# A fused attention and MLP block on one core: where the normed x is spilled, when Q is loaded, and how far the row maxima run ahead

## The chip, the cores and the metric

The kernel runs on one core of a Trainium2 chip. Its time is device microseconds (us) of the program; lower is better. The engines are named as in the profile: PE (TensorE matmul), PEld (its weight loads), DVE (VectorE), ACT (ScalarE), POOL (GpSimd) and SP (SyncE, which here issues nearly all DMA transfers, in order). SPq is the issuing side of SP.

## The reference

All in fp32, with x of [1, 2048, 512], 32 heads of 16, and an MLP of width 1792:

```python
def reference(A_x, A_wqkv, A_wo, B_x, B_w1, B_b1, B_w2, B_b2):
    xn = _layernorm(A_x)                                  # (x - mean) / sqrt(var + 1e-5)
    # attention on xn
    qkv = (xn @ A_wqkv)   # -> q, k, v, each [32 heads, 2048, 16]
    p = softmax(q @ k.T * 16 ** -0.5)
    s = (p @ v, heads joined) @ A_wo
    # MLP on xn
    h = relu(xn @ B_w1 + B_b1) ** 2
    g = silu(h @ B_w2 + B_b2)
    return A_x + s * g
```

## The kernel before

**Numbers.** Every fp32 operand is split into a high and a low part, and a product is three matmuls (high by high, high by low, low by high). On most tiles POOL makes the split (lines 93 and 94: the high part, then the remainder); some are split by ACT and DVE (99 and 100). Matmuls of the later stages use 64 rows of the array each, and two of them, on the upper and the lower half, run at the same time: such a couple is called a pair here, and a half a side or lane.

**Stages.** (1) To about 64 us: x is loaded, normed and transposed into four tiles `xT` (one for each 512 tokens, both parts, 2 MB each), and the first projections run. (2) The lead, from 64 to about 182 us: the other projections (V, Q, K). The function `side_rounds` walks through 390 rounds; a round is one matmul on each side; a projection tile takes 12 rounds a side, and the lower side runs 18 rounds behind. `single` puts extra matmuls between the rounds: 'm' is one tile of scores of which DVE takes the row maxima (line 321), 's' is one tile of exponentials on ACT (1195). The lists `ROUND_MM`, `ROUND_MS` and `ROUND_SM` say in which rounds. (3) The loop over 512 slots, 16 for each of 32 units (a unit is 4 heads by 512 queries). A slot has four tiles of exponentials, four of maxima for later units, the product with V (384) and a share of the MLP's matmuls (252) in groups of four slots ("long slots"), eight chunks of 256 tokens, 56 slots each. (4) From slot 452: the output projection (220), then the end.

**The maxima.** For the softmax the maxima over keys of a unit are taken ahead of its exponentials; `LEAD` = 24 slots separate the two, and each side takes 32 maxima a unit. Once a unit's 64 are there, `max_end` reduces them (329), and six slots later `shift` (351 to 354, on DVE) transposes and negates them; they go to DRAM (360) and come back (375) into two rows of the unit's Q tile, so that the score matmul subtracts them.

**A projection tile of Q or K** goes PSUM, ACT copy `raw` (1000, two buffers), POOL split into `hl` (93, 94, three buffers), then two DMA stores, one of the high and one of the low part (938). A V tile goes through ACT to `vt` (1040, seven buffers) and a store (1043). The order of SP, ACT, DVE and POOL is fixed by the order of the calls; `later(n, fn)` puts a call off by n steps: in the lead a step is six rounds, in the loop a slot.

**DMA around the change.** `load_q_pair` loads one Q tile with six DMAs of 32 KB (147); `qm` tiles serve the maxima (a ring of three), `qe` tiles the exponentials (four). `max_end(g)` calls it at set slots of each unit. The normed x is written from `xT` to DRAM in eight spills of 1 MB (1355), at every third slot count g of the lead, and is read back for the MLP by `load_xc` (497), as two DMAs for each chunk:

```python
            if s in (7, 8):
                load_q_pair(u, "qe", s - 7, qes.setdefault(u, []))
            if s in (5, 7) and u + 1 < NU:
                load_q_pair(u + 1, "qm", (s - 5) // 2, qms.setdefault(u + 1, []))
```

The first xc can only be loaded when the lead's last matmul has read `xT`, whose memory it takes. In the tail `wo_load` brings the attention outputs `oc` (667). POOL normalises a unit's outputs in slot 12 of the next unit (422 to 424), from a list of slots called `EVAC`.

Of the kernel before, what the change touches and what calls it, by code (L numbers as in the profile page):

```python
# [9 lines left out]
F32 = mybir.dt.float32  # L10
# [7 lines left out]
P = 128  # L18
S = 2048
D = 512  # L20
# [3 lines left out]
KO = D // P  # L24
# [3 lines left out]
NU = NQ * 4  # L28
LEAD = 24
CW = 256  # L30
# [5 lines left out]
EVAC_LAST = (1, 3, 4, 5, 7, 9)  # L36
GAPS = (18, 19, 20, 22)
FIRST = 2
LAST_MAX = 486
TWO = (2, 3, 452, 453)  # L40
ROUND_MM = [12 * k for k in range(1, 32)] + [12 * k + 6 for k in range(2, 22)]
ROUND_MS = [12 * k + 6 for k in (22, 23, 25, 26, 28, 29)]
ROUND_SM = [12 * k + 6 for k in (24, 27, 30)]
AHEAD = (
# [7 lines left out]
def kernel(  # L52
# [11 lines left out]
    nc = tc.nc  # L64
# [11 lines left out]
    xn_d = dram.tile([2, P, KO, S], F32, name="xn_d")  # L76
# [9 lines left out]
    b1_t = const.tile([P, FO], F32, name="b1_t")  # L86
    b2_t = const.tile([P, D], F32, name="b2_t")
# [21 lines left out]
    with ExitStack() as ph:  # L109
# [31 lines left out]
        qms = {}  # L141
        qes = {}
# [182 lines left out]
        def max_end(g):  # L325
            for u in [u for u, n in left.items() if n == 0]:
                del left[u]
                m4 = m4s[u % 2]
                nc.vector.tensor_reduce(m4[:, :16], mxs[u], axis=AX.X, op=ALU.max)
                mxs[u] = m4  # L330
                late.append((g + (6 if u else 2), u))
            u, s = divmod(g, 16)
            if u >= NU:
                return
            qd, qc = divmod(u, 4)
            if qc == 2 and qd + 1 < NQ and s % 2 == 0:
                load_k(qd + 1, s // 2)
            if qc == 3 and qd + 1 < NQ and s % 2 == 0 and s < 8:
                load_k(qd + 1, 8 + s // 2)
            if s in (7, 8):  # L340
                load_q_pair(u, "qe", s - 7, qes.setdefault(u, []))
            if s in (5, 7) and u + 1 < NU:
                load_q_pair(u + 1, "qm", (s - 5) // 2, qms.setdefault(u + 1, []))

        def shift_due(g):
            if late and late[0][0] <= g:
# [117 lines left out]
        def mlp_tasks(mp):  # L464
# [28 lines left out]

            def load_xc(c):
                    xc = xp.tile([P, 2, KO, CW], F32R, name="xc")
                    for i in range(2):
                        nc.sync.dma_start(
                            xc[:, i].bitcast(F32), xn_d[i, :, :, c * CW : (c + 1) * CW]
                        )
                    state["xc"] = xc  # L500

            def first_pair(c, f):
# [397 lines left out]
        st = right(ln, "wq_st", 1)  # L900
# [7 lines left out]
        xTs = {c: cp.tile([P, 2, KO, 512], F32R, name=f"xT{c}") for c in (3, 0, 1, 2)}  # L908
# [25 lines left out]
        def qk_store(m, c, hl):  # L934
            cs = slice(c * 512, (c + 1) * 512)
            dst = q_d[m] if m < 4 else k_d[m - 4]
            for i in range(2):
                nc.sync.dma_start(dst[i, :, cs], hl[:, i].bitcast(F32))

        def qk_terms(m, c, ps):  # L940
            wq, m0 = wq_cols(m)
# [217 lines left out]
        order = []  # L1159
# [58 lines left out]
        for i in range(NT + 3):  # L1218
            if i in (2, 3):

                kos = slice(2 * i - 4, 2 * i - 2)
# [35 lines left out]
            if i >= 7 and (i - 3) % 4 == 3:  # L1257
                c = (i - 3) // 4
# [3 lines left out]
            if i >= 3 and (i - 3) % 4 == 3:  # L1262
                c = (i - 3) // 4
# [48 lines left out]
        def lead_rounds():  # L1312
            for i in side_rounds(specs, single):
                if i % 6 == 0:
                    now[0] = i // 6
                    run_waiting()
                kinds = "mm" if i in ROUND_MM else "ms" if i in ROUND_MS else "sm" if i in ROUND_SM else ""
                uses = [single(lane, kind) for lane, kind in enumerate(kinds)]
                if i % (3 * KO) == 0 and uses:
                    since[0] = uses[0]  # L1320
                if i == 6 * KO:
                    since[1] = uses[1]
                yield

        rounds = lead_rounds()
        for g in range(LEAD):
            shift_due(g)
            while min(made) < 2 * g + 2:
                next(rounds)
            max_end(g)  # L1330
            if g == 0:
                raw_r = [load_w("wv", 3 * P, ((D + P, 3 * P),))]
            if g == 3:
                for ko in range(KO):
                    split_w(wr_t, ko, slice(3 * P, 6 * P), raw_r[0][:, ko])
                ln.close()
                pools["v"] = ph.enter_context(tc.tile_pool(name="vp", bufs=1))
            if g == 12:
                s1.close()
                ep = ph.enter_context(tc.tile_pool(name="ep", bufs=1))  # L1340
                rot["pt"] = [ep.tile([P, 512], F32, name=f"pt{i}") for i in range(NPT)]
                pools["n"] = ph.enter_context(tc.tile_pool(name="np", bufs=1))
                mlp_early()
            if g in (18, 20):
                split_w1((g - 18) // 2)
                load_w1(3 + (g - 18) // 2)
            if g == 16:
                for fo in range(3):
                    load_w1(fo)
                load_v(0)  # L1350
                nc.sync.dma_start(b1_t, b1.rearrange("(fo p) -> p fo", p=P), allow_slow_non_contiguous=True)
                nc.sync.dma_start(b2_t, b2[None, :].to_broadcast([P, D]))
            if g % 3 == 2:
                c, i = divmod(g // 3, 2)
                nc.sync.dma_start(
                    xn_d[i, :, :, c * 512 : (c + 1) * 512], xTs[c][:, i].bitcast(F32)
                )
        for _ in rounds:
            pass
        run_waiting(True)  # L1360
        assert made == [60, 60] and not [1 for it in to_exp for _ in it]
        lead.close()
        first.close()

# [39 lines left out]
        def slot(st, mms, post):  # L1404

            g = st + LEAD
            lane = (st + flip[0]) % 2
            kb0 = st - lane
            for kb in (kb0, kb0 + 1):
                pts.setdefault(kb, {})  # L1410
            spare = st >= LAST_MAX
            ex = [
                lambda j=j, kb=kb: exp_mm(kb, j, pts[kb], spare and next(odd))
                for kb in (kb0, kb0 + 1) for j in (1 - lane, 3 - lane) if j not in pts[kb]
            ]
            if st in TWO:

                for _ in range(2):
                    max_mm(lane)
                    ex.pop(0)()  # L1420
                if ex:
                    kb, j = (kb0 + 1, 2 + lane) if lane else (kb0, lane)
                    exp_mm(kb, j, pts[kb], True)
                    ex.pop(0)()
                last_use[0] = None
                max_end(g)
                return
            k = 0 if spare else max(0, (8 - len(mms)) // 2)
            own = [lambda: max_mm(lane) for _ in range(k)] + mms
            if spare and lane == 0:  # L1430

                own.append(lambda: exp_mm(kb0, 0, pts[kb0], next(odd)))
            mx = [] if spare else [lambda: max_mm(1 - lane) for _ in range(4 - k)]
            order = "s" * len(ex) if spare else {0: "smsmsmsm", 1: "smsmssm"}[k]
            if not spare and post is None:

                if k == 0:
                    order = "msmsmsms"
                elif lane and k == 1 and to_block:
                    order = "smsmsms"  # L1440
            other = [(ex if o == "s" else mx).pop(0) for o in order]
            other[-1:-1] = [None] * (len(own) - len(other))
            use = None
            for i in range(len(other)):
                if i < len(own):
                    own[i]()
                if spare and lane == 0 and i == len(mms) - 1:

                    use = nc.vector.tensor_scalar(seen, done_d[0][:, :1], 1.0, 0.0, op0=ALU.mult, op1=ALU.add)
                if other[i] is not None:  # L1450
                    follow = other[i]()
# [123 lines left out]
```

## Time and profile before

| What | Value |
|---|---|
| time, median of 3 runs | 1665.18 us (1664.69 to 1665.99) |
| the profiled execution's own time | 1664.16 us |
| its span | 1662.4 us |
| PE busy | 1628.7 us (98%) |
| DVE busy | 1363.0 us (82%) |
| ACT busy | 1192.8 us (72%) |
| POOL busy | 524.7 us (32%) |
| mean granted clock of PE | 0.995 |
| moved over DMA | 209.23 MB |

A line of a group or of the order in time reads: start and length in us, engine, line of the kernel, operation, output <- input, shapes, count, and in brackets the idle time ahead of it with what ended it. A line of the waits reads: who waited <- for whom, us in total, times, the longest. A line by stage has busy us and instructions of each engine, the granted clock, the share of the DMA engines that was busy, and GB/s. A busy PE is one in which some matmul is running, on one side or both.

### The profile page before, as it was taken

What the parts mean: (1) busy time and instruction counts of PE and PEld (TensorE: products, weight loads), DVE (VectorE), ACT (ScalarE), POOL (GpSimd) and SP (SyncE); (2) the same over time, 40 slices, a digit from 0 to 9 for tenths busy, and PEclk for the clock granted to TensorE, in tenths of its full rate; (3) what the DMA queues carried; (4) which work ended last, traced back from release to release, by engine and by line L of the source; (5) the groups of instructions that cost most, each with busy time, mean ns of one, the idle gap of its engine ahead of it and who ended that gap; (6) DMA issues with size and microseconds to landing.
All of it is one profiled execution on the core that took longest, in us unless ns stands there. A gap on an engine that the chain in (4) does not pass through costs nothing.

```text
span 1662.4 us, 36155 instructions
## 1 busy us (share of the span) xinstructions
PE 1628.7 (98%) x13684; PEld 939.1 (56%) x13684; DVE 1363.0 (82%) x2346; ACT 1192.8 (72%) x2351; POOL 524.7 (32%) x547
## 2 busy tenths in 40 slices
PE   8999799999999999999999999999999999999998
PEld 7887565556545654564466446645654565445443
DVE  6485588888888888888888888888888888887654
ACT  7312477777777777777777777777777777777686
POOL 6445467423212321231133103311331133216421
PEclk9999899999999999999999999999999999999999
DMA  6677655434333333333433244323532252245654
GB/s 224 196 257 237 211 173 152 120 91 145 83 85 101 116 85 91 105 111 79 107 99 96 73 106 123 107 70 88 139 96 67 76 155 76 66 136 177 186 178 153
DMA packets 164421, 209.23 MB, mean 126 GB/s; under 512 B 59928, under 2 KB 78872, under 8 KB 162712
## 3 DMA queue, kind: packets, MB, share of 16 engines
q1 hardware_dynamic: 163960, 206.40, 42.8%
q8 instruction: 108, 1.77, 0.5%
q14 instruction: 65, 0.53, 0.1%
q10 hardware_dynamic: 288, 0.52, 0.1%
HBM read 149.95 MB, written 56.61 MB: 124 GB/s over the span
## 4 chain that ended last, share of the span: by engine, by line
PE 93%; DMA 3%; DVE 2%; SPq 1%; issue 1%; POOL 1%; ACT 0%; POOLq 0%; DVEq 0%; ACTq 0%
PE po L384 30%; PE pd_t L252 18%; PE pm_t L314 17%; PE se L1183 14%; PE pd_t L220 5%; PE pm_t L1061 3%; PE se L1031 1%; PE se L983 1%; DVE mx L321 1%; PE pd_t L1061 1%; DMA q_d<-hl 1%; PE se L314 1%; DMA xr<-in_A_x_dram 1%; SPq L147 1%; PE pm_t L1183 1%
## 5 line engine op out<-in xcount | busy, mean ns | idle before, releaser
L321 DVE TENSOR_REDUCE mx<-pm_t 128x1 f32<-128x512 f32 x1931 | 1199.7, 684 | 182.6 <-PE pm_t L314 90.3
L1195 ACT ACTIVATE pt<-se 128x512 f32<-128x512 f32 x1996 | 1045.9, 615 | 273.3 <-PE se L1183 217.9
L314 PE MATMUL pm_t<-ka,qm 64*128 64x512 f32 x1931 | 775.7, 422 | 5.3 <-DVE mx L321 5.2
L1183 PE MATMUL se<-qe,ka 64*128 64x512 f32 x1996 | 673.6, 397 | 1.1 <-DVE mx L321 0.8
L384 PE MATMUL po<-pt,v 128*32 128x512 f32 x4096 | 546.2, 605 | 0.0
L314 PEld LDWEIGHTS pm_t<-ka,qm 64*128 64x128 f32 x1931 | 339.6, 184 | 249.6 <-DVE mx L321 234.8
L252 PEld LDWEIGHTS pd_t<-xc,w1s 64*128 64x128 f32 x2688 | 336.8, 187 | 97.6 <-issue 89.7
L252 PE MATMUL pd_t<-xc,w1s 64*128 64x256 f32 x2688 | 386.3, 290 | 3.2 <-DMA xc<-xn_d 3.2
L1183 PEld LDWEIGHTS se<-qe,ka 64*128 64x128 f32 x1996 | 337.5, 185 | 20.1 <-ACT pt L1195 1.2
L252 PE MATMUL pd_t<-w2t,hT 64*128 64x512 f32 x1080 | 301.5, 411 | 0.0
L252 PEld LDWEIGHTS pd_t<-w2t,hT 64*128 64x128 f32 x1080 | 178.9, 184 | 81.9 <-issue 75.5
L540 POOL TENSOR_TENSOR r<-r 128x512 f32<-128x512 f32 x56 | 58.4, 1042 | 381.5 <-ACT r L537 381.5
L384 PEld LDWEIGHTS po<-pt,v 128*32 128x32 f32 x4096 | 81.0, 108 | 158.7 <-issue 136.2
L559 POOL TENSOR_TENSOR u<-u,b_t 128x512 f32<-128x512 f32 x16 | 20.6, 1286 | 354.1 <-ACT u L558 354.1
L321 DVE TENSOR_REDUCE mx<-se 128x1 f32<-128x512 f32 x117 | 76.0, 687 | 36.6 <-PE se L314 27.8
L220 PE MATMUL pd_t<-wot,oc 64*128 64x512 f32 x336 | 91.9, 409 | 4.0 <-DMA oc<-on_d 4.0
L537 ACT ACTIVATE r<-pd_t,b_t 128x256 f32<-128x256 f32 x112 | 47.0, 471 | 57.1 <-PE pd_t L252 57.1
L422 POOL TENSOR_TENSOR ot<-ot,hl 128x512 f32<-128x512 f32 x31 | 40.0, 1290 | 151.8 <-DMA hl<-r_d 151.6
L220 PEld LDWEIGHTS pd_t<-wot,oc 64*128 64x128 f32 x336 | 58.6, 185 | 50.8 <-ACT pt L1195 12.6
L1061 PE MATMUL pm_t<-xT,wr_t 64*128 64x512 f32 x408 | 77.1, 400 | 0.0
L94 POOL TENSOR_TENSOR hT<-r,hT 128x512 fp32r<-128x512 f32 x56 | 72.4, 1293 | 4.7
L220 PE MATMUL pd_t<-w2t,hT 64*128 64x512 f32 x264 | 69.2, 394 | 0.0
(131 smaller groups left out, 1078.7 us busy)
## 6 DMA issues: line engine op xcount, KB each, us to landing
w1s<-w_d SPq DMA_DIRECT2D x196, 256.0 KB
qm<-q_d SPq DMA_DIRECT2D x384, 32.0 KB
ka<-k_d SPq DMA_DIRECT2D x96, 128.0 KB
qe<-q_d SPq DMA_DIRECT2D x384, 32.0 KB
k_d<-hl SPq DMA_DIRECT2D x32, 256.0 KB
q_d<-hl SPq DMA_DIRECT2D x32, 256.0 KB
xn_d<-xT SPq DMA_DIRECT2D x8, 1024.0 KB
xc<-xn_d SPq DMA_DIRECT2D x16, 512.0 KB
```

Of the source, the lines that this page charges most:

```text
L94: (lo or nc.gpsimd).tensor_tensor(dst[1], raw, dst[0].bitcast(F32), op=ALU.subtract)
L220: mm = nc.tensor.matmul(out_, lh(r), rh(r), start=first_ and lane == 0, stop=last_ and lane == 1, skip_group_check=True,)
L252: mm = nc.tensor.matmul(out_, lh(r), rh(r), start=first_ and lane == 0, stop=last_ and lane == 1, skip_group_check=True,)
L314: nc.tensor.matmul(ps, qms[u][p][64 * j : 64 * j + 64, qb * P : (qb + 1) * P], kas[qd, p][64 * j : 64 * j + 64, kc * 512 : (kc + 1) * 512] ...
L321: return nc.vector.tensor_reduce(mxs[u][:, c, kc : kc + 1], ps, axis=AX.X, op=ALU.max)
L384: nc.tensor.matmul(po[32 * j : 32 * j + 32, :], vs[qd][:, (4 * kb + j) * VW : (4 * kb + j) * VW + 32], pts[j], start=(kb == 0), stop=(kb = ...
L422: nc.gpsimd.tensor_tensor(ot, ot, hl[:, 1].bitcast(F32), op=ALU.mult)
L537: nc.scalar.activation(r[:, i], ps[:, i * CW : (i + 1) * CW], AF.Relu, bias=b1_t[:, fo : fo + 1])
L540: nc.gpsimd.tensor_tensor(r, r, r, op=ALU.mult)
L1061: mm = nc.tensor.matmul(out_, lh(r), rh(r), start=first_ and lane == first, stop=last_ and lane != first, skip_group_check=True,)
L1183: nc.tensor.matmul(se, kas[qd, j // 2][b : b + 64, kb * P : (kb + 1) * P], qes[u][j // 2][b : b + 64, :], start=True, stop=True,)
L1195: return nc.scalar.activation(pts[j], se, AF.Exp, scale=0.25)
```

## The change

- **Spills.** The eight spills of the normed x leave the slots g = 2, 5, ... 23 and are issued at the steps `SPILLS` of the lead. The loads of b1 and b2 move from g = 16 to step 26.
- **Stores.** A projected Q or K tile is written by one DMA of 512 KB instead of two of 256 KB.
- **Q loads.** `qe` pairs are loaded in slots 12 and 14 of a unit instead of 7 and 8 (unit 0 stays), `qm` pairs in slots 6 and 10 instead of 5 and 7.
- **Maxima.** Rounds 6 and 18 of the lead get two more maxima each, so that with the slots 2 and 3 each side has 64 ahead of slot 4, the first long one; slots 484 and 485 have two fewer each.
- **The first xc** is loaded in four pieces of 256 KB, two for ko 0 and 1, then two for ko 2 and 3.

```diff
+SPILLS = (4, 7, 10, 13, 15, 17, 19, 21)
+PAIR = (484, 485)
-ROUND_MM = [12 * k for k in range(1, 32)] + [12 * k + 6 for k in range(2, 22)]
+ROUND_MM = [12 * k for k in range(1, 32)] + [12 * k + 6 for k in range(22)]
...
-            if s in (7, 8):
-                load_q_pair(u, "qe", s - 7, qes.setdefault(u, []))
-            if s in (5, 7) and u + 1 < NU:
-                load_q_pair(u + 1, "qm", (s - 5) // 2, qms.setdefault(u + 1, []))
+            at = (12, 14) if u else (7, 8)
+            if s in at:
+                load_q_pair(u, "qe", at.index(s), qes.setdefault(u, []))
+            if s in (6, 10) and u + 1 < NU:
+                load_q_pair(u + 1, "qm", s // 10, qms.setdefault(u + 1, []))
...
-                    for i in range(2):
-                        nc.sync.dma_start(
-                            xc[:, i].bitcast(F32), xn_d[i, :, :, c * CW : (c + 1) * CW]
-                        )
+                    for k in (0, 2) if c == 0 else (0,):
+                        kos = slice(k, k + 2 if c == 0 else KO)
+                        for i in range(2):
+                            nc.sync.dma_start(
+                                xc[:, i, kos].bitcast(F32), xn_d[i, :, kos, c * CW : (c + 1) * CW]
+                            )
...
-            for i in range(2):
-                nc.sync.dma_start(dst[i, :, cs], hl[:, i].bitcast(F32))
+            nc.sync.dma_start(dst[:, :, cs].rearrange("i p n -> p i n"), hl.bitcast(F32))
...
+                    if i // 6 in SPILLS:
+                        c, k = divmod(SPILLS.index(i // 6), 2)
+                        nc.sync.dma_start(
+                            xn_d[k, :, :, c * 512 : (c + 1) * 512], xTs[c][:, k].bitcast(F32)
+                        )
+                    if i // 6 == 26:
+                        nc.sync.dma_start(
+                            b1_t, b1.rearrange("(fo p) -> p fo", p=P), allow_slow_non_contiguous=True
+                        )
+                        nc.sync.dma_start(b2_t, b2[None, :].to_broadcast([P, D]))
...
-            if g % 3 == 2:
-                c, i = divmod(g // 3, 2)
-                nc.sync.dma_start(
-                    xn_d[i, :, :, c * 512 : (c + 1) * 512], xTs[c][:, i].bitcast(F32)
-                )
...
-            mx = [] if spare else [lambda: max_mm(1 - lane) for _ in range(4 - k)]
+            mx = [] if spare else [lambda: max_mm(1 - lane) for _ in range(2 if st in PAIR else 4 - k)]
...
+            if st in PAIR:
+                order = "smsmss"
```

More of the change, by code (lines that the diff above doesn't have):

```diff
@@ L1350 @@
                 load_v(0)
-                nc.sync.dma_start(b1_t, b1.rearrange("(fo p) -> p fo", p=P), allow_slow_non_contiguous=True)
-                nc.sync.dma_start(b2_t, b2[None, :].to_broadcast([P, D]))
-            if g % 3 == 2:
-                c, i = divmod(g // 3, 2)
-                nc.sync.dma_start(
-                    xn_d[i, :, :, c * 512 : (c + 1) * 512], xTs[c][:, i].bitcast(F32)
-                )
         for _ in rounds:
@@ L1360 @@
         run_waiting(True)
-        assert made == [60, 60] and not [1 for it in to_exp for _ in it]
+        assert made == [62, 62] and not [1 for it in to_exp for _ in it]
         lead.close()
@@ L1432, in slot @@
                 own.append(lambda: exp_mm(kb0, 0, pts[kb0], next(odd)))
-            mx = [] if spare else [lambda: max_mm(1 - lane) for _ in range(4 - k)]
+            assert k == 0 or st not in PAIR
+            mx = [] if spare else [lambda: max_mm(1 - lane) for _ in range(2 if st in PAIR else 4 - k)]
             order = "s" * len(ex) if spare else {0: "smsmsmsm", 1: "smsmssm"}[k]
```

## The prediction

> **What bounds the kernel now.** I read the page first, then the list of what TensorE (PE) waited for, then the busy time by stage, then the order in time of PE, SP, POOL and DVE around each wait. The page, its summary by engine and its PE row:
>
> ```profile
> PE 1628.7 (98%) x13684; PEld 939.1 (56%) x13684; DVE 1363.0 (82%) x2346; ACT 1192.8 (72%) x2351; POOL 524.7 (32%) x547
> PE   8999799999999999999999999999999999999998
> ```
>
> PE is idle for 1662.4 - 1628.7 = 33.7 us of the span. An edit that takes no matmul away can win only that, and the time in which PE runs at a lower clock after an idle stretch. The change reaches these waits (total us, times, longest):
>
> ```profile
> PE se L314 <- ACT pt L1195: 7.2, 2, 5.1
> PE pm_t L314 <- DVE mx L321: 5.2, 8, 0.9
> PE pd_t L220 <- DMA oc<-on_d: 4.0, 1, 4.0
> PE pd_t L252 <- DMA xc<-xn_d: 3.2, 2, 1.9
> PE se L1183 <- DVE mx L321: 0.8, 1, 0.8
> ```
>
> The stages of the lead (projections with the first maxima; columns: stretch, length, then busy us and instructions of PE, PEld, DVE, ACT, POOL, granted clock, DMA share, GB/s), and one 5 us slice:
>
> ```profile
> 61.00:100.00 39.00, 39.00 (x321) 34.24 (x322) 29.16 (x46) 9.73 (x17) 8.54 (x9) 1.00 0.54 192
> 100.00:130.00 30.00, 30.00 (x266) 25.92 (x264) 24.81 (x42) 5.39 (x9) 18.28 (x22) 1.00 0.88 299
> 130.00:160.00 30.00, 27.13 (x218) 22.79 (x216) 16.34 (x26) 7.82 (x14) 16.91 (x22) 0.94 0.82 265
> 160.00:185.00 25.00, 19.51 (x140) 14.27 (x141) 10.96 (x18) 7.95 (x15) 13.21 (x17) 0.86 0.71 239
> 106.00:111.00 5.00, 5.00 (x46) 4.32 (x46) 3.87 (x6) 0.60 (x1) 1.95 (x3) 1.00 1.03 382
> ```
>
> The DMA engines are half idle to 100 us, full from 100 on, and PE starves from 130 to 185, where also the clock falls. How that comes about (PE, then POOL and ACT, then SP's issues):
>
> ```profile
> 147.98 0.49 PE L314 MATMUL se<-ka,qm 64*128 64x512 f32 x1 [2.07 <-ACT pt L1195]
> 149.90 3.14 PE L1061 MATMUL pm_t<-xT,wr_t 64*128 64x512 f32 x12
> 174.51 0.79 PE L314 MATMUL se<-ka,qm 64*128 64x512 f32 x1 [5.08 <-ACT pt L1195]
> 162.44 1.29 POOL L94 TENSOR_TENSOR hl<-raw,hl 128x512 fp32r<-128x512 f32 x1
> 171.37 0.62 POOL L93 TENSOR_SCALAR hl<-raw 128x512 fp32r<-128x512 f32 x1 [7.64 <-DMA k_d<-hl]
> 173.37 0.60 ACT L1000 ACTIVATE raw<-pm_t 128x512 f32<-128x512 f32 x1 [7.58 <-POOL hl L94]
> 158.69 3.16 SPq L147 DMA_DIRECT2D qe<-q_d  x6
> 161.95 3.30 SPq L147 DMA_DIRECT2D qm<-q_d  x6
> 165.29 0.53 SPq L1355 DMA_DIRECT2D xn_d<-xT  x1
> 165.92 1.67 SPq L938 DMA_DIRECT2D k_d<-hl  x2
> ```
>
> Read upwards from the bottom: the store of a projected tile stands in SP's order behind twelve Q loads (6.6 us) and a 1 MB spill; its buffer `hl` (three of them) comes free only at 171.37; POOL waits, ACT's eviction waits for POOL, the exponentials queued behind it on ACT wait, and PE waits 5.08 us for a bank. The wait of 2.07 us is the same chain.
>
> **A: the lead.** The spills leave the slots g = 2, 5, ... 23 and go into the sixth-rounds 4 to 21. In the built order of SP all eight now come before the first of the last 24 tile stores, where six stood among them; the stores are one issue each instead of two; b1 and b2 go behind the third of them, not the eighth; of the Q loads among them 12 (qm2, qe2) go behind the xc loads. PE's order changes only by four more maxima, at rounds 6 and 18. The durations:
>
> ```profile
> 76.57 0.64 SPq L1355 DMA_DIRECT2D xn_d<-xT  x1
> 64.19 0.50 PE L1061 MATMUL pm_t<-wa_t,xT 64*128 64x512 f32 x1
> 130.38 1.32 PE L1061 MATMUL pm_t<-xT,wr_t 64*128 64x512 f32 x10
> 131.99 1.32 PE L1061 MATMUL pm_t<-xT,wr_t 64*128 64x512 f32 x10
> 181.15 0.62 PE L1061 MATMUL pd_t<-xT,wr_t 64*128 64x512 f32 x2
> 66.00:71.00 5.00, 5.00 (x45) 3.83 (x43) 4.65 (x8) 0.46 (x2) 0.00 (x0) 1.00 0.48 181
> 176.00:181.00 5.00, 5.00 (x30) 3.89 (x28) 0.30 (x2) 1.56 (x3) 3.13 (x3) 0.58 0.43 159
> ```
>
> From 130.38 to 131.99 lie six rounds and one extra pair of maxima: 1.61 / 7 = 0.230 us per pair of matmuls on the two halves of the array. The lead has 390 rounds and 60 extra pairs: 103.5 us, so from 64.19 it would end at 167.7; it ends at 181.77, with 14.1 lost. Named of these: idle 0.8 + 2.07 + 5.08 = 8.0; the twelve matmuls after the first stall take 3.14 where ten take 1.32 and twelve would take 1.55, so 1.6 lost; after the second the clock is 0.58 and 30 matmuls stand in a slice that holds 45, 1.7, and 0.7 for the slow pairs before 176, so 2.4. Together 12.0.
>
> Do the stores get through now? The four stages moved 7.5 + 9.0 + 8.0 + 6.0 = 30.4 MB; over 106 us that is 287 GB/s, where the slice at 106 shows 382. The crowd is early: the second spill now stands in SP's order where the first stood, behind the V stores (issued at 76.57), so some seven spills (7.3 MB) and at most 3.4 MB else lie between 76 and 101, 28 us at 382 GB/s: drained at about 105. The first store behind them is due at 101; it lands some 5 us late, and three `hl` and two `raw` at one tile in 3.2 us (14 pairs) cover that. After 105 the stores need 0.52 MB in 3.2 us, 164 GB/s. So I let all 12.0 go. Next late is DVE: the first 18 rounds now hold ten maxima, not eight, and round 18 two more; eight take DVE 4.65 us, 0.58 each, and there are three banks, so the twelfth needs nine done, 0.9 (two rounds and a matmul) + 9 x 0.6 = 6.3 us after the start, where PE would be at 5.0 (22 pairs). I charge 1.4, and 0.5 for two more pairs. A = 12.0 - 1.9 = **10.1**, from 2.6 (one stall stays, 5.08 + 2.4) to 12. The four maxima taken from slots 484 and 485 give nothing: their other half of the array carries nine output matmuls, and still does.
>
> **B: the first xc.**
>
> ```profile
> 182.84 1.29 SPq L497 DMA_DIRECT2D xc<-xn_d  x2
> 188.10 0.35 PE L252 MATMUL pd_t<-xc,w1s 64*128 64x256 f32 x1 [1.85 <-DMA xc<-xn_d]
> 189.81 0.38 PE L252 MATMUL pd_t<-xc,w1s 64*128 64x256 f32 x1 [1.36 <-DMA xc<-xn_d]
> ```
>
> PE is there at 186.25; the high halves land at 188.10, the low ones at 189.8, and every product needs both. In four pieces the first 512 KB hold ko 0 and 1 of both: the second wait goes, but for some 0.2, as ko 2 is needed 1.4 us later. With fewer stores queued ahead I let the first wait shrink from 1.85 to 1.2. If so, the slow stretch behind it goes too, which I price as that behind the 2.07 us wait, 1.6; a wait of 0.8 us left none. B = 3.2 - 1.4 + 1.6 = **3.4**; bounds 1.2 (1.85 and 0.2 stay, and the clock falls) and 4.8. The Trainium skill, TensorE: Matmul & The Clock Gate, section Part 1: The HAM clock gate, has the clock fall after an idle window of about 3.4 us; by that the 1.6 were never lost, B would be 1.8 and the sum 1.6 less, but here 2.07 us of idling were enough, so the trace decides. The Trainium skill's DMA: Bandwidth & Descriptors, section Anatomy of one DMA, gives each transfer a fixed 2.0 us besides bytes / 436 GB/s: it speaks against four pieces where the queue is empty, yet two of 256 KB would then land some 3.9 us after the first issue (an estimate from it), ahead of PE, for a B of 4.8; no run here shows a lone piece.
>
> **C: the shifts in the loop.** With 64 maxima a side ahead of slot 4, the last maximum of a unit falls on the end of a group of four slots, and the transpose and negation of its maxima, six slots later, move from the boundary of slots 11 and 12 (modulo 16) to that of 8 and 9. At slot 12 POOL starts to normalise a unit's outputs:
>
> ```profile
> 354.78 1.22 DVE L354 SCALAR_TENSOR_TENSOR sh<-tr,sh 128x32 fp32r<-128x32 f32 x1
> 354.66 1.30 POOL L422 TENSOR_TENSOR ot<-ot,hl 128x512 f32<-128x512 f32 x1
> ```
>
> DVE's small operation ends where POOL's ends (356.0). While it hangs the maxima stop and PE waits 0.9 us; this recurs every seven units, four times, 3.6 us; the other four of the eight waits (5.2 - 3.6 = 1.6 us) lie ahead of them, in the lead's end and the first MLP chunk. At slot 9 POOL's work from the group before (about 3 us from the middle of slot 7) is over, but in the first chunk it also splits weights then, so I leave those four. C = **3.6**, between 1.5 and 4.9. The Trainium skill's SBUF — State Buffer, section SBUF: two separate sides, calls this pair of ports an exclusive lock held for the whole instruction; by that and by the rows alike a collision costs up to one POOL operation.
>
> **D: the tail.**
>
> ```profile
> 1504.97 0.62 SPq L360 DMA_DIRECT2D sh_d<-sh  x1
> 1512.92 2.11 SPq L375 DMA_DIRECT2D qe<-sh_d  x4
> 1516.92 3.52 SPq L147 DMA_DIRECT2D qm<-q_d  x6
> 1537.31 0.78 SPq L667 DMA_DIRECT2D oc<-on_d  x1
> 1541.87 0.61 PE L220 MATMUL pd_t<-wot,oc 64*128 64x512 f32 x1 [3.98 <-DMA oc<-on_d]
> ```
>
> SP stands 7.3 us for the shift's round trip and then issues four blocks of six Q loads before the oc for which PE waits. Three of the blocks now stand behind it, some 9 us, so it is issued near 1528, lands near 1533, and PE needs it at 1537.9. The 3.98 go, and 1.6 of slow clock as above: D = **5.5**, from 2 (the moved Q loads delay the next oc) to 5.6. In the loop the Q loads are still ten slots (28 us) ahead of use.
>
> The sum: 10.1 + 3.4 + 3.6 + 5.5 = 22.6. The profiled execution took 1664.16 us, so 1641.6; it stands 1.0 under the median of the runs, 1665.18, so I forecast **1642.6**.
>
> **The rivals.** (1) The lead keeps one stall. SP still stands for the shift of unit 0 near 125 us with w1 and V loads in the queue; if the stores behind it come over 6 us late, 5.08 + 2.4 come back: 1650. For it: 7 us of such a stand in the tail; against: three `hl` and two `raw`. (2) The spills weren't the cause; SP's order and its Q loads were, and the lead gains nothing but pays its 1.9: B to D less 1.9 is 10.6: 1654.6. For it: the twelve Q loads stand right ahead of the 5.08; against: they take 6.6 us of SP, and the buffer came free 9 after POOL's last use. (3) Slower: eight spills within 30 us back up all that follows, and each tile from 98 us on finds no `hl`. It decides when a store takes more than 6.4 us (two `raw` at 3.2) beyond its turn, as after 165. Each such tile costs up to 5.08 + 2.4 = 7.5; four of them, 30, outrun the gain: 1673. For it: 10.7 MB in 25 us is over 382 GB/s; against: the backlog is 5 us, once, and the stage from 100 to 130, with its slice at 382, passed without PE idling.
>
> **How the numbers follow.** The forecast 0.76, (1) 0.12, (2) 0.07, (3) 0.05. The forecast's own range by the bounds is 1638 to 1648. To hold 8 in 10 I go from 1638 to 1651, which takes in (1). About 0.2%, 3.3 us, is what a measurement of this kernel can tell from none. Faster 0.94 (forecast, 1 and 2, less 0.01), same 0.01, slower 0.05.
>
> **What would show it.** Right: PE at clock 1.00 from 64 to the lead's end near 170; no wait of L314 for ACT; DMA nearly full from 76 to 105; a DVE-bound second near 67; no 1.22 us on L354 in the later chunks; no wait for oc. Wrong: POOL waiting for q_d or k_d stores over 6 us before 135, a wait for oc elsewhere in the tail, or a shift that meets POOL at another slot.

## The result, and the profile after

| | before | after |
|---|---|---|
| median | 1664.93 us (1662.84 to 1665.99) | **1646.4 us** (1644.67 to 1649.4) |
| ratio of the times | | 0.989 (95%: 0.987 to 0.991) |
| the profiled execution, its span | 1664.16, 1662.4 us | 1644.67, 1642.6 us |

The change wins 18.5 us between the medians and 19.5 between the profiled executions; 22.6 were forecast, and the time lies in the range of 1638 to 1651. But the parts of the sum are not those of the forecast. In all files after, lines stand some lines lower (L314 is L316, L384 is L387, and so on). First the page's row of engines, to lay beside that of before:

```profile
PE 1619.3 (99%) x13684; PEld 940.6 (57%) x13684; DVE 1359.5 (83%) x2346; ACT 1190.1 (72%) x2351; POOL 523.0 (32%) x547
```

The same 13684 matmuls keep PE busy for 9.4 us less (1628.7 to 1619.3), and its idle time falls from 33.7 to 1642.6 - 1619.3 = 23.3, 10.4 less. So half of the gain was never idle time. What PE waited for in after, the waits that the forecast is about (total us, times, longest):

```profile
PE pd_t L222 <- DMA oc<-on_d: 3.5, 1, 3.5
PE se L316 <- ACT pt L1199: 2.4, 1, 2.4
PE pd_t L254 <- DMA xc<-xn_d: 0.8, 2, 0.6
PE pd_t L254 <- POOL w1s L96: 0.8, 1, 0.8
PE se L1187 <- DMA qe<-sh_d: 0.6, 1, 0.6
PE pm_t L316 <- DVE mx L323: 0.5, 1, 0.5
```

The two waits for ACT in the lead shrank to one of 2.4, and a new one of 0.6 for qe<-sh_d came up; those for the maxima and for xc are nearly gone, and the wait for oc is still there. To see which stretch won what, the loop needs marks that both kernels have: once a unit, ACT copies its output out of PSUM (`ot<-po`, 30 of them). The first of these copies and the 26th, in before and then in after:

```profile
232.09 0.62 ACT L394 ACTIVATE ot<-po 128x512 f32<-128x512 f32 x1
1382.90 0.62 ACT L394 ACTIVATE ot<-po 128x512 f32<-128x512 f32 x1
```

```profile
222.56 0.62 ACT L397 ACTIVATE ot<-po 128x512 f32<-128x512 f32 x1
1362.61 0.62 ACT L397 ACTIVATE ot<-po 128x512 f32<-128x512 f32 x1
```

| stretch, profiled executions | before | after | won | forecast |
|---|---|---|---|---|
| start to first copy (A and B) | 232.09 | 222.56 | 9.5 | 13.5 |
| first to 26th copy (C) | 1150.81 | 1140.05 | **10.8** | 3.6 |
| 26th to last mark (D) | 267.03 | 267.33 | **-0.3** | 5.5 |

The last mark is ACT's copy of the last unit, `tot<-po` of 128x256, at 1649.93 and 1629.94. In the loop PE was idle for 4.6 us before and for nothing after; the other 6.2 us of the 10.8 won there were busy time, with the same 10027 matmuls (stretch, length, then busy us of each engine, clock, DMA share, GB/s; before, then after):

```profile
232.09:1382.90 1150.81, 1146.23 (x10027) 635.99 (x10025) 1018.13 (x1726) 885.23 (x1756) 311.70 (x317) 1.00 0.38 105
222.56:1362.61 1140.05, 1140.04 (x10027) 635.12 (x10025) 1013.87 (x1726) 882.37 (x1756) 310.45 (x317) 1.00 0.38 105
```

The lead alone in after, in stages and in the slice where DVE should become the bound (66 to 71):

```profile
61.00:100.00 39.00, 38.80 (x309) 34.52 (x310) 30.12 (x48) 9.34 (x17) 7.05 (x7) 1.00 0.78 266
100.00:130.00 30.00, 30.00 (x265) 26.96 (x264) 25.07 (x42) 5.77 (x10) 16.58 (x20) 1.00 0.82 274
130.00:160.00 30.00, 27.00 (x220) 24.89 (x218) 16.71 (x27) 7.02 (x13) 19.19 (x25) 0.94 0.76 245
160.00:185.00 25.00, 22.69 (x190) 18.57 (x190) 15.55 (x26) 11.54 (x23) 16.74 (x21) 1.00 0.63 218
66.00:71.00 5.00, 4.80 (x32) 2.91 (x32) 5.00 (x10) 0.00 (x0) 0.00 (x0) 1.00 1.05 404
```

The traffic is moved ahead (192 to 266 GB/s up to 100). The last stage has 190 matmuls, not 140, at clock 1.00, not 0.86; it now holds more of the first MLP chunk, as the lead ends at 175 and not at 182. Between 130 and 160 PE still starves, with 220 matmuls where 218 stood. From 66 to 71 DVE is busy for all 5.00 us and PE does 32 matmuls, not 45.

### The profile page after: what moved, and what is told of

The parts are those of the page before. It is cut to its first block, busy times and chain, and to the rows that moved or that the text cites. A ratio compares the mean times of both kernels' runs of the same rounds, so it can differ in the third digit from the quotient of the medians.

```text
span 1642.6 us, 36131 instructions
## 1 busy us (share of the span) xinstructions
PE 1619.3 (99%) x13684; PEld 940.6 (57%) x13684; DVE 1359.5 (83%) x2346; ACT 1190.1 (72%) x2351; POOL 523.0 (32%) x547
## 4 chain that ended last, share of the span: by engine, by line
PE 96%; DMA 2%; DVE 1%; SPq 0%; issue 0%; ACT 0%; DVEq 0%; ACTq 0%
PE po L387 31%; PE pd_t L254 19%; PE pm_t L316 16%; PE se L1187 14%; PE pd_t L222 6%; PE pm_t L1065 3%; PE se L1035 1%; PE pd_t L1065 1%; PE se L987 1%; PE se L316 1%; DVE mx L323 1%; DMA oc<-on_d 1%; PE pm_t L1187 0%; DMA sh_d<-sh 0%; PE pm_t L1149 0%; PE pd_t L1035 0%
## 5 line engine op out<-in xcount | busy, mean ns | idle before, releaser
L316 PE MATMUL pm_t<-ka,qm 64*128 64x512 f32 x1927 | 770.5, 420 | 0.7 <-DVE mx L323 0.5
L387 PE MATMUL po<-pt,v 128*32 128x512 f32 x4096 | 546.1, 605 | 0.0
L316 PEld LDWEIGHTS pm_t<-ka,qm 64*128 64x128 f32 x1927 | 338.5, 184 | 239.0 <-DVE mx L323 226.8
L254 PE MATMUL pd_t<-xc,w1s 64*128 64x256 f32 x2688 | 380.9, 288 | 1.7 <-DMA xc<-xn_d 0.8
L387 PEld LDWEIGHTS po<-pt,v 128*32 128x32 f32 x4096 | 81.0, 108 | 159.1 <-issue 136.5
```

Of the source, the lines that this page charges most:

```text
L254: mm = nc.tensor.matmul(out_, lh(r), rh(r), start=first_ and lane == 0, stop=last_ and lane == 1, skip_group_check=True,)
L316: nc.tensor.matmul(ps, qms[u][p][64 * j : 64 * j + 64, qb * P : (qb + 1) * P], kas[qd, p][64 * j : 64 * j + 64, kc * 512 : (kc + 1) * 512] ...
L387: nc.tensor.matmul(po[32 * j : 32 * j + 32, :], vs[qd][:, (4 * kb + j) * VW : (4 * kb + j) * VW + 32], pts[j], start=(kb == 0), stop=(kb = ...
```

## The experiments

The column "first copy" is the end of A and B; "loop" the first to the 26th copy; "28 to 30" the stretch of the tail where PE waits for oc. Times are medians, and each ratio is to runs of before taken beside that kernel; shift7 and shift10 ran once only. The stretches are those of one profiled execution each.

| kernel | time | ratio to before (95%) | first copy | loop | 28 to 30 |
|---|---|---|---|---|---|
| before | 1664.93 | 1 | 232.09 | 1150.81 | 107.60 |
| after | 1646.4 | 0.989 (0.987 to 0.991) | 222.56 | 1140.05 | 107.23 |
| max_only | 1652.47 | 0.992 (0.990 to 0.993) | 234.54 | 1140.45 | 104.07 |
| spill_only | 1660.68 | 0.997 (0.996 to 0.998) | 227.25 | 1151.30 | 108.83 |
| q_only | 1660.68 | 0.997 (0.996 to 0.998) | 226.27 | 1150.67 | 109.33 |
| late_shift | 1667.25 | 1.0005 (0.999 to 1.002) | 225.21 | 1150.64 | 107.80 |
| shift7 | 1660.01 | one run | 223.91 | 1148.04 | 110.76 |
| shift10 | 1658.82 | one run | 225.11 | 1140.11 | 114.41 |
| before_next | 1655.74 | 0.995 (0.993 to 0.997) | 232.59 | 1141.54 | 107.86 |
| loads13 | 1646.58 | 0.988 (0.987 to 0.990) | 222.80 | 1140.04 | 108.46 |
| tail_q | 1641.28 | 0.986 (0.984 to 0.987) | 226.03 | 1139.93 | 101.87 |
| xc2 | 1647.74 | 0.989 (0.987 to 0.991) | 226.52 | 1139.90 | 108.04 |
| two_stores | 1645.6 | 0.988 (0.987 to 0.990) | 225.40 | 1139.86 | 107.49 |
| **best** | **1639.36** | 0.985 (0.983 to 0.986) | 221.25 | 1139.95 | 101.88 |

**The parts alone.** max_only: the kernel before with the two earlier maxima a side and nothing else.

```diff
+PAIR = (484, 485)
-ROUND_MM = [12 * k for k in range(1, 32)] + [12 * k + 6 for k in range(2, 22)]
+ROUND_MM = [12 * k for k in range(1, 32)] + [12 * k + 6 for k in range(22)]
...
+            mx = [] if spare else [lambda: max_mm(1 - lane) for _ in range(2 if st in PAIR else 4 - k)]
...
+            if st in PAIR:
+                order = "smsmss"
```

> The kernel before with the two earlier maxima a side (rounds 6 and 18, slots 484 and 485 with two fewer) and nothing else of the change. Measured from the first copy of a unit's outputs out of PSUM to the 26th, the loop took 1150.8 us before and 1140.1 after. Theory S (the shift's small DVE operations met POOL's normalising at slot 12, and with 64 maxima a side ahead they no longer do): 1140 to 1141, so 10 us less. Theory R (the loop's gain comes from the Q loads being spread): 1150 to 1151. In the lead both expect the stalls of before (2.1 and 5.1 us) and about 1.5 us more at its start, where DVE must take two more maxima a side. Total by S about 1656, by R about 1667.

The loop's gain is there in full (1140.45), with no spill or Q load moved; the first copy comes 2.4 later, and the stretch from 28 to 30 is 3.5 shorter. So the maxima, meant for 3.6, win most of the change.

spill_only: the spills at the steps `SPILLS`, all else as before.

```diff
+SPILLS = (4, 7, 10, 13, 15, 17, 19, 21)
+                    if i // 6 in SPILLS:
...
-            if g % 3 == 2:
...
```

> The kernel before with only the eight spills moved to the early steps. Theory L (the spills among the tile stores starved PE in the lead): the wait of 5.1 us goes and the one of 2.1 us with it, first copy of a unit's outputs at 222 to 226 us where before had 232.1 and after 222.6; total about 1656 to 1659. Rival (the twelve Q loads right ahead of that store and SP's order are the cause): a wait of several us for ACT stays between 160 and 180, first copy at 229 to 232, total 1662 to 1665. Loop from the first to the 26th copy unchanged at 1150.8 by both.

q_only: the Q loads at their new slots, all else as before.

```diff
-            if s in (7, 8):
+            at = (12, 14) if u else (7, 8)
...
-            if s in (5, 7) and u + 1 < NU:
+            if s in (6, 10) and u + 1 < NU:
```

> The kernel before with only the Q loads in their new slots. Theory S: loop from the first to the 26th copy at 1150 to 1151 as before. Theory R: 1140 to 1144. In the tail PE's wait for oc (4.0 us near 1540 before, 3.5 near 1495 after): if the wait moved because two blocks of six Q loads now stand in front of the output projection's own transfers, it is here as in the kernel after, 3 to 4 us near the 29th copy and none at the 30th; if the shift's earlier place moved it, it stays near 1540. In the lead 12 Q loads fewer among the last stores: the 5.1 us wait shrinks to 1 to 3 if those loads hold up the store, stays at 5 if the spills alone do. Total 1657 to 1665.

Either one takes the wait of 5.08 away, and brings the first copy forward by 4.8 and 5.8. Their waits, spill_only first, then q_only:

```profile
PE se L1184 <- DMA qe<-sh_d: 4.5, 1, 4.5
PE se L315 <- ACT pt L1196: 1.2, 2, 0.7
```

```profile
PE pd_t L220 <- DMA oc<-on_d: 4.2, 1, 4.2
PE se L314 <- ACT pt L1196: 2.2, 1, 2.2
```

With the spills moved alone, unit 0's maxima come back 4.5 us late, so less is won than was expected (1660.68 us, not 1656 to 1659). With the Q loads moved alone one wait for ACT of 2.2 stays, and the wait for oc moves to an earlier unit, as in after (its stretch from copy 28 to 29 grows from 49.13 to 56.71, the next shrinks from 58.47 to 52.62).

**What in the maxima's order wins.** The next kernels put the shift of a unit (transpose and negation) at other slots of after. late_shift: nine slots after the last maximum, so back at the boundary of 11 and 12.

```diff
-                late.append((g + (6 if u else 2), u))
+                late.append((g + (9 if u else 2), u))
```

> The kernel after, but the shift of a unit's maxima comes nine slots after the last maximum, not six, so that it stands at the boundary of slots 11 and 12 again, where POOL normalises; everything else as after. Theory S: the loop from the first to the 26th copy is back at 1149 to 1151 (after: 1140.1), the small DVE operation takes up to 1.2 us again, total 1654 to 1658. If the gain came from anything else than the place of the shift (the last maximum on a group's end, the Q loads): 1140 to 1142 and a total of 1645 to 1648.

The loop is that of before again (1150.64): the slot of the shift is the cause, 10.6 us of it, three times what POOL's collision was to cost. Most of the rest of its loss, which was not expected, lies in the tail, where the maxima come back too late (a wait of 4.8 for qe<-sh_d). shift7 and shift10 (7 and 10 in place of 9) were to part the collision with POOL from the slot itself:

> The kernel after, with the shift seven slots after the last maximum, at the boundary of slots 9 and 10. POOL does nothing there in most units, but slot 10 opens with five maxima where slot 9 holds three. The loop from the first to the 26th copy took 1140.1 us after and 1150.6 with the shift at the boundary of 11 and 12. If the collision with POOL is all of that difference: 1140 to 1141. If part of it is that the shift stands ahead of a slot with five maxima, so that DVE falls behind and PE finds no bank for 0.2 to 0.3 us a unit: 1145 to 1147, every unit but those in which no group of four slots runs some 0.27 us longer, and none of the four steps of 1.2.

> The kernel after, with the shift ten slots after the last maximum, at the boundary of slots 12 and 13: POOL is still normalising, but slot 13 holds three maxima, not five. If the collision is all: 1148 to 1152 for the loop from the first to the 26th copy. If the number of maxima behind the shift is the larger part: 1140 to 1145, with DVE's small operation still drawn out to 0.5 us or more on average. The rows that the shift writes may then come late for the unit's first exponentials, which would show as a wait of L1187 for qe<-sh_d, to be taken off.

shift7, at the boundary of 9 and 10, still loses 8.0 us of loop (1148.04). shift10, at 12 and 13, loses none (1140.11); its time of 1658.82 comes from the tail, where the maxima come back too late (waits of 6.2 us in all for qe<-sh_d, 5.1 for oc). Neither is free of POOL, though shift7 was expected to be. In shift7 four shifts meet the normalising, which itself starts when its load has landed; in shift10 four meet POOL's work behind it, but are drawn out less than in late_shift. A pair of lines for shift7, then a shift of late_shift and one of shift10:

```profile
935.30 1.29 POOL L425 TENSOR_TENSOR ot<-ot,hl 128x512 f32<-128x512 f32 x1 [25.74 <-DMA hl<-r_d]
935.55 1.07 DVE L356 TENSOR_SCALAR sh<-tr 128x32 fp32r<-128x32 f32 x1
```

```profile
668.87 1.22 DVE L357 SCALAR_TENSOR_TENSOR sh<-tr,sh 128x32 fp32r<-128x32 f32 x1
668.68 0.55 DVE L357 SCALAR_TENSOR_TENSOR sh<-tr,sh 128x32 fp32r<-128x32 f32 x1
```

So the totals alone do not part the two causes, but the single units do. From one copy to the next, each kernel against after (us longer):

| kernel | maxima behind the shift | four units whose shift meets POOL | the other 21, mean |
|---|---|---|---|
| before | five | 1.24 to 1.29 | 0.27 |
| late_shift | five | 1.28 to 1.32 | 0.26 |
| shift7 | five | 0.46 to 1.12 | 0.24 |
| shift10 | three | 0.02 to 0.06 | 0.00 |

A shift that POOL leaves alone already costs about 0.26 us a unit in the first three, some 6.5 us in 25 units; each of the four collisions of 1.22 us adds about 1.0, some 4 us in all. The 0.26 does not go by the distance from the last maximum: it is there at six, seven and nine slots, and not at six (after) and ten. What differs is how many maxima stand behind the shift: three in after and shift10, five in before, late_shift and shift7. before_next tries that on the kernel before, by one number, at seven slots as in shift7:

```diff
-                late.append((g + (6 if u else 2), u))
+                late.append((g + (7 if u else 2), u))
```

> The kernel before with one number changed: the transpose and negation of a unit's maxima come seven slots after the last maximum, not six, so at the boundary of slots 12 and 13 (modulo 16), ahead of a slot with three maxima and not ahead of one with five; no spill, store, Q load or maximum is moved. POOL normalises there too. If what follows the shift decides, the loop from the first to the 26th copy falls from 1150.8 us to 1140 to 1141.5, as in the changed kernel, and the time by 8 to 11 to 1654 to 1657. If instead it is the meeting with POOL or the two earlier maxima a side that count, the loop stays at 1147 to 1151 and the time at 1661 to 1666. The round trip of the maxima is one slot shorter before use, which can cost 0 to 5 us in the tail by either.

The loop falls to 1141.54, the ratio to 0.995 (0.993 to 0.997), though POOL draws four of its shifts out to 0.55 as in shift10. DVE's order in time shows why; an ordinary unit of before, then of before_next:

```profile
717.09 3.08 DVE L321 TENSOR_REDUCE mx<-pm_t 128x1 f32<-128x512 f32 x5 [0.19 <-PE pm_t L314]
720.72 1.89 DVE L321 TENSOR_REDUCE mx<-pm_t 128x1 f32<-128x512 f32 x3 [0.55 <-PE pd_t L252]
722.52 0.20 DVE L351 STREAM_TRANSPOSE tr<-m 128x32 f32<-128x32 f32 x1
723.12 3.08 DVE L321 TENSOR_REDUCE mx<-pm_t 128x1 f32<-128x512 f32 x5
726.69 1.89 DVE L321 TENSOR_REDUCE mx<-pm_t 128x1 f32<-128x512 f32 x3 [0.49 <-PE pd_t L252]
```

```profile
718.70 3.08 DVE L321 TENSOR_REDUCE mx<-pm_t 128x1 f32<-128x512 f32 x5 [0.20 <-PE pd_t L252]
721.70 0.20 DVE L351 STREAM_TRANSPOSE tr<-m 128x32 f32<-128x32 f32 x1
722.33 1.88 DVE L321 TENSOR_REDUCE mx<-pm_t 128x1 f32<-128x512 f32 x3
```

Five and three maxima alternate, with 0.2 us of DVE idling ahead of the five and 0.55 ahead of the three in these rows. The shift takes 0.6 (722.52 to 723.12). Ahead of three maxima it falls into the larger gap; ahead of five, the five end late, and PE, whose maxima wait for one of three banks, slows. In before this shows in the spacing of the maxima's matmuls, 0.56 and 0.59 us where 0.46 is usual:

```profile
723.30 0.40 PE L314 MATMUL pm_t<-ka,qm 64*128 64x512 f32 x1
723.86 0.50 PE L314 MATMUL pm_t<-ka,qm 64*128 64x512 f32 x1
724.45 0.50 PE L314 MATMUL pm_t<-ka,qm 64*128 64x512 f32 x1
```

Matmuls of the other half run meanwhile, so this is no idle time of PE, and PE's list of waits does not hold it. The list of the weight loads does: from the first copy to the 26th, those of the maxima waited 206.3 us for DVE in before, 198.1 in after. (late_shift and shift7 have 205.7 and 206.0, shift10 and before_next 198.0 and 199.4.)

```profile
PEld pm_t L314 <- DVE mx L321: 206.3, 304, 1.1
PEld pm_t L316 <- DVE mx L323: 198.1, 292, 0.9
```

**The lead.** loads13: in after, the w1 and V loads at g = 13 and not at 16.

```diff
-            if g == 16:
+            if g == 13:
```

> The kernel after, with the first three w1 loads and the first V load at slot count g = 13 of the lead instead of 16, so that SP issues them ahead of the shift of unit 0 by some 9 us and the round trip of the shift has a shorter queue in front. If SP's stand for that round trip (130 to 136.4 us) is what starves PE at 140 to 145: the 2.4 us wait for ACT and the 0.6 us for qe<-sh_d go, the first copy comes at 218 to 220 us (after: 222.6), total 1642 to 1645. If the tile stores are late for another reason: 222 to 223, total as after, 1645 to 1648.

The waits of 2.4 and 0.6 go, and the lead is 3 us shorter. So the one stall that the lead kept was this chain of after: SP issues w1, stands for unit 0's maxima to come back (129.99 to 136.4), POOL waits 5.82 for the store that stands behind, ACT waits for POOL, PE for ACT:

```profile
127.11 2.15 SPq L452 DMA_DIRECT2D ex<-in_B_w_dram  x3
129.99 3.94 SPq L363 DMA_DIRECT2D sh_d<-sh  x1
136.37 2.24 SPq L378 DMA_DIRECT2D qe<-sh_d  x4
138.72 0.38 SPq L942 DMA_DIRECT2D k_d<-hl  x1
141.72 0.62 POOL L95 TENSOR_SCALAR hl<-raw 128x512 fp32r<-128x512 f32 x1 [5.82 <-DMA k_d<-hl]
143.73 0.60 ACT L1004 ACTIVATE raw<-pm_t 128x512 f32<-128x512 f32 x1 [7.20 <-POOL hl L96]
144.87 0.79 PE L316 MATMUL se<-ka,qm 64*128 64x512 f32 x1 [2.43 <-ACT pt L1199]
145.00:147.00 2.00, 2.00 (x10) 2.00 (x12) 0.69 (x1) 0.00 (x0) 1.83 (x4) 0.50 0.67 258
```

But the time did not follow (1646.58): between the lead's end and the first MLP chunk the clock fell to 0.50 in loads13 and not in the profiled after. The slices from 182 to 186 of loads13 and after:

```profile
182.00:186.00 4.00, 4.00 (x25) 2.11 (x22) 1.87 (x3) 1.79 (x3) 0.00 (x0) 0.50 0.32 75
```

```profile
182.00:186.00 4.00, 3.33 (x32) 2.05 (x30) 2.52 (x4) 2.36 (x5) 0.00 (x0) 1.00 0.35 86
```

It fell in the other kernels with the earlier spills and Q loads too. In slices of 0.5 us the stretch at 0.50 lasts 3.4 us in best (180.1 to 183.5), two_stores, late_shift and shift7, and 6.8 in loads13 (179.6 to 186.5), tail_q, xc2 and shift10; earlier in the lead it lasts 3.4 at the stall of 2.43 in after, and in before 3.4 at the one of 2.07 and 6.8 at that of 5.08. Best in its slow stretch and behind it:

```profile
180.50:183.00 2.50, 2.46 (x17) 2.46 (x18) 1.38 (x2) 0.95 (x2) 0.00 (x0) 0.50 0.19 34
183.50:186.00 2.50, 2.50 (x23) 1.08 (x26) 1.11 (x3) 1.01 (x2) 0.00 (x0) 1.00 0.28 66
```

xc2 (the first xc in two DMAs of 512 KB) and two_stores (two DMAs a projected tile), each in after:

```diff
-                    for k in (0, 2) if c == 0 else (0,):
+                    for k in (0,):
...
```

> The changed kernel, but the first xc comes in two DMAs of 512 KB (high, low), as before, and not in four of 256 KB. If the four pieces are what cut the waits for the first xc (3.2 us before, 0.8 in two waits of at most 0.6 after), two waits come back, 2.5 to 3.2 us together, one of them at the low halves, and the first MLP matmuls end their waiting 1 to 2 us later: a time 1 to 3 us above the changed kernel's 1646.4, so 1647.5 to 1649.5, first copy of a unit's output 1 to 3 us later at a like clock. If the emptier queue alone did it (the stores end earlier now), the waits stay under 1.2 us and the time at 1646. Loop (1140.1 from the first to the 26th copy) and tail (107.2 from the 28th to the 30th) as in the changed kernel by both.

```diff
-            nc.sync.dma_start(dst[:, :, cs].rearrange("i p n -> p i n"), hl.bitcast(F32))
+            for i in range(2):
+                nc.sync.dma_start(dst[i, :, cs], hl[:, i].bitcast(F32))
```

> The changed kernel, but a projected Q or K tile is written by two DMAs of 256 KB again. If one store a tile matters because SP issues less, the 24 last tiles cost SP 0.5 to 0.8 us more each, the wait of PE for ACT in the lead (2.4 us) grows by 1 to 3 and the qe<-sh_d wait of 0.6 to 1 to 4 (as the 4.5 us with the spills moved alone), and the first copy comes 1 to 5 us later: 1647 to 1651. If SP has room in the lead, all stays as it was: waits for ACT of 2 to 3 us, 1646. Loop 1140 and tail 107 as in the changed kernel by both.

xc2 brings both waits for xc back (3.5 us in all, against 0.8), and the clock falls to 0.57 from 182 to 190: the pieces do what B says of them. The time is 1647.74 against 1646.4, a difference inside the spread of either. The single store does nothing that shows in the time: with two it is 1645.6, and the wait for ACT is 2.5 as in after; only that for qe<-sh_d is 1.6, not 0.6.

**The tail.** tail_q: in after, the Q loads of unit 29 alone at their old slots.

```diff
-            at = (12, 14) if u else (7, 8)
+            at = (12, 14) if u and u != 29 else (7, 8)
...
+                am = (6, 10) if u != 29 else (5, 7)
```

> The kernel after, with the Q loads asked for in unit 29's slots back at the slots of before, so that no block of six Q loads stands between the first transfers of the output projection. From the 28th copy to the 30th: 107.6 us before, 107.2 after, 104.1 with the earlier maxima alone. If the moved Q loads brought the 3.5 us wait for oc near 1495: 102 to 104, no wait over 2 us there, total 1642 to 1645. If the wait has another cause (the sum of bytes in the tail): 107 and 1646.

The wait for oc is gone, and the stretch from copy 28 to 30 falls by 5.4, though the first copy came 3.5 later in this profile (6.8 us of slow clock, where the profiled after had none there). In after two blocks of Q loads stand in SP's order ahead of the oc of 1474.80; in tail_q they go before, and it is issued at 1471.27; counted from the 28th copy, that is 20.7 us behind it in after and 13.9 in tail_q. After, then tail_q:

```profile
1458.48 3.66 SPq L672 DMA_DIRECT2D oc<-on_d  x6
1466.47 2.75 SPq L149 DMA_DIRECT2D qe<-q_d  x6
1471.29 3.00 SPq L149 DMA_DIRECT2D qe<-q_d  x6
1474.80 0.43 SPq L672 DMA_DIRECT2D oc<-on_d  x1
1495.05 0.50 PE L222 MATMUL pd_t<-wot,oc 64*128 64x512 f32 x1 [3.54 <-DMA oc<-on_d]
```

```profile
1454.40 2.68 SPq L149 DMA_DIRECT2D qe<-q_d  x6
1461.39 2.95 SPq L673 DMA_DIRECT2D oc<-on_d  x6
1471.27 0.43 SPq L673 DMA_DIRECT2D oc<-on_d  x1
```

Which of the oc loads was late, and whether by its issue or by the Q traffic beside it, these runs do not part.

best joins the two edits, of loads13 and tail_q:

> The changed kernel with the Q loads of unit 29 at their old slots (7 and 8, 5 and 7) and the w1 and V loads of the lead at g = 13, not 16: the two edits that each took away a wait. If they add up, the wait for ACT in the lead (2.4 us) and the tail's wait for oc (3.5 us, with the length from the 28th to the 30th copy at 102, not 107) are both gone; by the tail's edit alone the time is 1641.3, and 0 to 3 us of the lead come on top: 1638.5 to 1641.5. If the time won in the lead is lost again in the slow clock between the lead's end and the first MLP chunk, as with the loads at g = 13 alone (1646.6), it stays at 1641 to 1642.

It is the fastest of all, 1639.36 us, 7 under after: the tail's 5.4 in full, and in the lead neither stall. Its interval and that of tail_q (1641.28) overlap, so that the loads at g = 13 add something on top is likely, not shown.

## Why the prediction was right, and where not

The total held because errors of size cancelled: C was worth 7.2 more than forecast, D 5.8 less, A and B together 4.0 less. That is luck in part: without the 7.2, which no term of the forecast foresaw, the time would lie near 1653.6, outside the range.

**A, 10.1 forecast.** The lead ran from 64.19 to 181.77 before and from 63.70 to 175.1 after, 117.6 against 111.4 us: 6.2 won. The start cost was right: 13 matmuls are missing from 66 to 71, 1.5 us against 1.4, with DVE the bound. The step that failed is "I let all 12.0 go": a stall of 2.43 stayed, with 0.57 ahead of it and a clock of 0.50 behind it. That is rival 1 by its mechanism, SP standing for unit 0's shift with w1 and V in the queue, at less than its price (5.08 + 2.4); POOL waited 5.82 for the store, where the rival asked for over 6. Where the w1 and V loads move out of its way, in best, the lead lasts 64.17 to 172.22, 108.05: 9.5 won, near the forecast. The DMA engines were not nearly full from 76 to 105 (0.77, at 269 GB/s and not the 382 that the forecast let drain the spills), but did not need to be.

**Rival 2** was half right: q_only wins 5.8 to the first copy without touching a spill, spill_only 4.8 without touching a Q load. The chain at 174 had two causes in one queue, and either cure was enough for the long wait.

**Rival 3** did not come: POOL's longest wait for a store before 130 was 5.83 us, at 114.80, and the buffers covered it: PE is busy for 30.00 of the 30 us from 100 to 130.

**B, 3.4.** From the lead's end to the first copy it is 232.09 - 181.77 = 50.32 before and 222.56 - 175.11 = 47.45 after, 2.9 won; with A's 6.2 and a lead that began 0.5 sooner these are the 9.5. The waits for xc went from 3.2 to 0.8; a wait for POOL's split of w1 of 0.8 came up beside them. The slow stretch behind the waits goes in some executions and stays in others (none in the profiled after, 3.4 or 6.8 us at clock 0.50 in others), and with it up to some 3 us of the first copy: after and tail_q differ in nothing before the tail, and their profiled executions by 3.5 us there (222.56 and 226.03). That is most of the spread of after's runs (4.7). So the 1.6 that B let go for the clock was won by the profiled execution, but not by the change alone. The Trainium skill's DMA: Bandwidth & Descriptors, section Anatomy of one DMA, from which B has its 2.0 us, gives that fit for transfers that GpSimd issues. SP issued these, and no run here shows a lone piece.

**C, 3.6.** The mechanism that C prices was right, and its size too: the four units with a collision lose 1.24 to 1.29 us in before against after, the others 0.27, so the four collisions were about 4.0. What C lacks is the larger part, some 6.8 us: five maxima behind every shift, whether POOL meets it or not. The step that failed is the bound at the start, that only idle time and slow clock can be won; 6.2 of C's 10.8 were busy time.

**D, 5.5.** The step that failed is "three of the blocks now stand behind it": they do, for that oc, but blocks moved from slots 7 and 8 to 12 and 14 land ahead of an earlier one; the wait came at 1495.05, 3.54 long. It was named as the bound below (2, the next oc is delayed) and as a sign of being wrong, but the order of SP was not followed for each oc. The -0.3 lies below even that bound.

On the clock: the Trainium skill, TensorE: Matmul & The Clock Gate, section Part 1: The HAM clock gate, lets the clock fall after an idle window of about 3.4 us that runs freely. The slow stretches here, 3.4 us or twice that, fit a window of that length. What the rows do not bear out is that as much idling is needed for the fall: 2.43 us, with 0.57 some time ahead, were enough in after, and in loads13 waits of 1.11, 0.28 and 0.61, while after held with 0.75, 0.24 and 0.56. That tail_q fell where after, with the same code up to there, did not, does fit a window that does not start with the idling.

## What to carry to other kernels

Where two halves of the array work at once, compare the length of equal slots or units, and read the waits of the weight loads beside those of the matmuls: a stream that is late on one half shows as longer spacing of its matmuls, and 0.26 us a unit, some 6.5 in all, was more here than any stall. In this kernel a small operation on the engine that is nearly full (DVE, busy for 1018 of the loop's 1151 us) belonged ahead of the slot with the least work for that engine, and moving it by one slot took one number and won 0.5%. When loads are moved in an in-order queue, go through every urgent load behind their new place, not only the one that waited.

## What the runs showed of the hardware

- The shift's operations on DVE, of 0.18 to 0.26 us when alone, took up to 1.22 us beside one of POOL. With five maxima behind it that cost about 1.0 us (before, late_shift); drawn out to 0.55 only, with three behind it, it cost nothing (shift10: 0.02 to 0.06). A full collision ahead of three shows in one unit only, from the 26th copy to the 27th: 45.87 to 45.92 us in after and six other kernels, whose shift is drawn out to 0.98 or 0.99 there, against 45.37 in shift10, about 0.5 us.
- The slow stretches of the clock lasted 3.4 or 6.8 us, at 0.50, wherever one was measured (the list is with loads13). Waits of 1.11, 0.28 and 0.61 us within 4 us brought 6.8 (loads13), waits of 1.10, 0.37 and 0.65 brought 3.4 (best), and 0.75, 0.24 and 0.56 none (after): what follows a short gap can't be told from its length alone.
- Six DMAs of 32 KB take SP 2.7 to 3 us to issue in the tail of after, and 4.2 to 5.7 in its lead (at 100.07 and 108.53): the same block of Q loads holds up what stands behind it up to twice as long there.
